# Weight sums of the blocks in more buffers, and the second mixture's words moved behind the second sum and the first gate

## The chip, the cores and the metric

One core of a Trainium2 chip runs the kernel. The metric is device time in microseconds (us) of one execution, the median of three. The engines named below are TensorE (PE, the matmuls; PEld are its weight loads), VectorE (DVE), ScalarE (ACT), GpSimd (POOL) and SyncE (SP), which here only issues DMAs.

## The reference

Attention in chunks of 64 feeds a gated layer (the first mixture, `_moe_ref`), and that feeds a second layer with a softmax and a norm (`_moe2_ref`).

```python
x = attention(q, k, v)                    # 4608 tokens x 512
h = x @ w_in                              # 512 x 2048
g = h * np.clip(h + 3.0, 0.0, 6.0) / 6.0
x = g @ w_out                             # 2048 x 512
h = x @ w_in2                             # 512 x 1024
solu = h * softmax(h)
y = (solu - mean) / sqrt(var + 1e-6) * g_ln @ w_out2
```

## The kernel before

Float32 products are made of three matmuls on split operands: each operand is a high part `hi` (a cast to fp32r) and a low part `lo` (the rest), and hi*hi, lo*hi and hi*lo are summed in PSUM. The 4608 tokens are nine blocks of 512.

The first three blocks run the first mixture directly. In the loop over `F` (two blocks of 16 hidden chunks each, from about 112 us to 308 us of the profile), `moe_h` makes a hidden chunk, `moe_gate_there` gates it on DVE, `moe_split` splits it (ACT casts `g_hi`, DVE subtracts `g_lo`), and `o_next` multiplies the chunk before by `wo`. Attention of later blocks runs in the same loop. Beside them the loop prepares weights for the later blocks, which use a seven-product (Strassen-like) form. `sums_of(kind, j)` adds the halves of two weight tiles on DVE (line 1075, into `w[0]` and `w[1]`) and forms four sums on POOL (lines 1080 to 1083). Two passes later, `split_sums(kind, j, i)` casts `w[i]` on ACT into a high part (line 1089), subtracts on POOL (line 1090), and `store_sums` writes both parts to memory. The table `UNITS` says in which pass a unit starts: input weights ("i", j) in passes 0, 2, ... 14, output weights ("o", j) in 1, 5, 7 and then in 16 to 24.

The last six blocks are three pairs. The third, `pair`, runs from 640 us to 760 us of the profile, in eight iterations of j. An iteration makes seven products `mul7` (A11, S2, S1, S3, A12, A22, S4) and, from j = 1, two `o_next`. Its sums are `u2` (line 1522, from S2), `u3` and `c22` (1532, 1534), `c21` (1552, from A22) and `c12` (1558, from S4); `gated` makes a rectified copy on ACT (line 1230) and multiplies on DVE (line 550). S3 adds to the bank that `u2` reads, so it waits for `u2`; A22 in the same way waits for `u3`; A11 of the next iteration takes the bank that `gated(a)` reads; S2 of the next iteration takes the bank that `c21` reads.

`fill` (class `Second`) prepares the weights of the second layer inside the pair, in windows. A window of words waits for a raw chunk from memory (`fetch`, into `xr0` and `xr1` in turn), scales it on ACT (line 155) and joins its words on DVE (lines 258, 261 and, for `w_out2`, 267). Its small steps are DVE subtractions: `lo` parts (line 295) and differences (302). `hi` casts on ACT into a free place (line 319). The places are few: `wi14`, `wi15`, `pbd`, and `s3` with `xo3`. `fill.store()` issues the stores of finished parts from ACT's own queue (line 326); a cast into a place waits until the stores of what it held have landed. All engines run their instructions in the order of the program, and a DMA that an engine issues stands in that order too.

Of the kernel before, what the change touches and what calls it, by code (L numbers as in the profile page):

```python
# [8 lines left out]
F32 = mybir.dt.float32  # L9
# [7 lines left out]
P = 128  # L17
# [4 lines left out]
def tile_kernel(  # L22
# [15 lines left out]
    NT, DM = out.shape  # L38
# [28 lines left out]
    xrp = ctx.enter_context(tc.tile_pool(name="xr", bufs=1))  # L67
    ap1 = ctx.enter_context(tc.tile_pool(name="ap1", bufs=1))
# [8 lines left out]
    def work_tile(tag, dtype=F32, shape=(P, DM), name=None):  # L77
        i = turns[tag] % width[tag]
        turns[tag] = i + 1
        return wcp.tile(list(shape), dtype, tag=f"{tag}{i}", name=name or tag)  # L80
# [263 lines left out]
    def load_2(n):  # L344

        o, j = LOADS[n]
        if o == "out":
            homes = ((ap2, "v"), (ap2, "v")), ((ap2, "p"), (ap2, "p")), ((ap1, "q"), (ap1, "tx0")), ((ap1, "tx1"), (ap1, "tx2"))
            t = out_w[j] = [narrow(*h) for h in homes[j]]
            for i in range(2):  # L350
                nc.sync.dma_start(out=t[i].bitcast(F32), in_=st2[OPERANDS.index((o, j))][:, i])
        else:
            t = wi_slot(2 * XQ.index(o) + j, F32R)
            w2[o, j] = pair_of(t)
            nc.sync.dma_start(out=t.bitcast(F32), in_=st2[OPERANDS.index((o, j))])
# [23 lines left out]
    def att_psum():  # L379
        return ps_att.tile([P, 2, DM], F32, tag="att", name="att")  # L380
# [4 lines left out]
    def h_psum():  # L385
        return ps_h.tile([P, DM], F32, tag="h", name="hp")
# [162 lines left out]
    def moe_gate(hp, t):  # L549
        nc.vector.scalar_tensor_tensor(  # L550
            out=t, in0=t, scalar=6.0, in1=hp, op0=ALU.min, op1=ALU.mult
        )

    def moe_split(t, eng, between=None):
        g_hi = gp.tile([P, BT], F32R, tag="g_hi", name="g_hi")
        g_lo = gp.tile([P, BT], F32R, tag="g_lo", name="g_lo")
        nc.scalar.copy(out=g_hi, in_=t)  # L557
        if between:
            between()
        eng.tensor_sub(out=g_lo, in0=t, in1=g_hi.bitcast(F32))  # L560
        return g_hi, g_lo
# [503 lines left out]

    def sums_of(kind, j):

        if kind == "o" and j < 3:
            t = xrp.tile([P, 2, DM], F32, tag="xr0", name="xr0")
            w = [t[:, i] for i in range(2)]  # L1070
        else:
            w = [ap1.tile([P, DM], F32, tag=f"tx{i}", name=f"tx{i}") for i in range(2)]
        for i in range(2):
            t = (wi if kind == "i" else wo)[2 * j + i].bitcast(F32)
            nc.vector.tensor_add(out=w[i], in0=t[:, 0], in1=t[:, 1])
        k = slice(0, 2 * P), slice(2 * P, DM)
        (a11, a12), (a21, a22) = ([t[:, c] for c in k] for t in w)
        if kind == "o":
            a12, a21 = a21, a12
        nc.gpsimd.tensor_add(out=a22, in0=a21, in1=a22)  # L1080
        nc.gpsimd.tensor_sub(out=a21, in0=a11, in1=a21)
        nc.gpsimd.tensor_sub(out=a11, in0=a22, in1=a11)
        nc.gpsimd.tensor_sub(out=a12, in0=a12, in1=a11)
        summed[kind, j] = w
# [74 lines left out]
    def mul7(ps, j, wn, xname, start, stop):  # L1159
        w, (hi, lo) = ring_take(wn, j), xq[xname]  # L1160
        n = 0
        for i, x in ((0, hi), (1, hi), (0, lo)):
            for kk in range(2):
                nc.tensor.matmul(  # L1164
                    ps, w[:, i, kk * P : (kk + 1) * P], x[:, kk],
                    start=(start and n == 0), stop=(stop and n == 5), skip_group_check=True,
                )
                n += 1
        ring_fetch()
# [54 lines left out]
    def o_next():  # L1224
        if pend:
            moe_o(*pend.pop(0))

    def gated(h):
        t = gp.tile([P, BT], F32, tag="t", name="t")
        nc.scalar.activation(out=t, in_=h, func=AF.Relu, bias=three[:])  # L1230
        moe_gate(h, t)
        return t

    def load_h(f):
        h_t2[f] = work_tile("s")
        nc.sync.dma_start(out=h_t2[f], in_=held[f])
# [253 lines left out]
    def load_o(f):  # L1490
        j, i = divmod(f, 2)
        wo[f] = wo_slot(f, F32R)
        for c in range(2):
            nc.sync.dma_start(
                out=halves_of(wo[f][:, c]), in_=sto[4 + 2 * i : 6 + 2 * i, j, :, c].rearrange("s p c -> p s c")
            )

    def pair(p, todo):
        b1, b2 = FIRST + 2 * p, FIRST + 2 * p + 1
        hang, fill = None, second[0]  # L1500
        for j in range(NJ):
            lastj = j == NJ - 1
            if j == 1:
                width.update({"s": 3, "xo": 3})
                fill.places.append(3)
            for f in range(2 * j + ND, 2 * j + ND + 2):
                if f < NF:
                    load_o(f)
            a = att_psum()[:, 0]
            mul7(a, j, "A11", "B11", True, False)  # L1510
            s1 = work_tile("s")
            nc.scalar.copy(out=s1, in_=a)
            if hang:
                t, f = hang
                g = moe_split(t, nc.gpsimd)
                pend.append((b1, f, g))
            if j:
                fill.window(1, 0)
            b = h_psum()
            mul7(b, j, "S2", "T2", True, False)  # L1520
            u2 = work_tile("s")
            nc.vector.tensor_add(out=u2, in0=s1, in1=b)  # L1522
            while todo:
                todo.pop(0)()
            if j:
                fill.window(1, 2)
            c = h_psum()
            mul7(c, j, "S1", "T1", True, False)
            o_next()
            mul7(b, j, "S3", "T3", False, False)  # L1530
            u3 = ap1.tile([P, DM], F32, tag="tx2", name="tx2")
            nc.vector.tensor_add(out=u3, in0=s1, in1=b)
            c22 = work_tile("xo")
            nc.vector.tensor_add(out=c22, in0=u3, in1=c)
            if not lastj:
                nc.sync.dma_start(out=held[2 * j + 1], in_=c22)
            if not j:
                fill.window(1, 0)
            mul7(a, j, "A12", "B21", False, True)
            if lastj:  # L1540
                for n in range(4):
                    load_2(n)
                fetch_x2(0)
            fill.store()
            t = gated(a)
            g = moe_split(t, nc.gpsimd)
            o_next()
            pend.append((b1, 2 * j, g))
            fill.window(0, 2 * (j > 0), False)
            mul7(b, j, "A22", "T4", False, True)  # L1550
            c21 = ap1.tile([P, DM], F32, tag=f"tx{j % 2}", name=f"tx{j % 2}")
            nc.vector.tensor_add(out=c21, in0=s1, in1=b)
            mul7(c, j, "S4", "B22", False, True)
            if lastj:
                for n in range(4, 8):
                    load_2(n)
            c12 = work_tile("xo")
            nc.vector.tensor_add(out=c12, in0=u2, in1=c)
            if lastj:
                h_t2[2 * j], h_t2[2 * j + 1] = c12, c22  # L1560
                for f in range(2):
                    load_h(f)
            else:
                nc.sync.dma_start(out=held[2 * j], in_=c12)
            fill.store()
            hang = gated(c21), 2 * j + 1
            if not j:
                fill.window(1, 2)
        g = moe_split(hang[0], nc.vector)
        pend.append((b1, hang[1], g))  # L1570

        es_r.close()
        xp[0] = ctx.enter_context(tc.tile_pool(name="xp", bufs=2, reuse_waits="tile"))
        width.update({"s": 4, "xo": 4})
        order = [NF - 1, NF - 2] + list(range(NF - 2))
        nxt = gated(h_t2.pop(order[0]))
        for i, f in enumerate(order):
            t = nxt
            if i == 1:
                o_next()  # L1580
            if i + 1 < NF:
                nxt = gated(h_t2.pop(order[i + 1]))
            if i != 1:
                o_next()
            g = moe_split(t, nc.vector)
            pend.append((b2, f, g, i))
            if i + 4 < NF:
                load_h(order[i + 4])
            end_work(i)
        flush()  # L1590
# [31 lines left out]
    for f in range(NF):  # L1622
# [4 lines left out]
        hp, t = moe_h(f, *xn[0])  # L1627
# [49 lines left out]
    for F in range(2 * NF):  # L1677
        b, f = 1 + F // NF, F % NF
        if F == 0:
            xn[2] = new_x()  # L1680
        hp, t = moe_h(f, *xn[b])
# [170 lines left out]
```

## Time and profile before

| | us |
|---|---|
| median of three runs (lowest, highest) | 1187.03 (1186.27, 1187.85) |
| the profiled execution's own time | 1183.92 |
| its span, first to last instruction | 1181.8 |
| PE busy in the span | 1167.3 |
| DVE, ACT, POOL busy | 886.8, 726.5, 490.9 |

The span is 2.1 us shorter than the profiled execution's time, and that time is 3.1 us below the median of the runs. Busy PE is 99% of the span, at a granted clock of 1.000 of full speed throughout.

### The profile page before, as it was taken

The page shows a single profiled execution, that of the slowest core. Times are in us where ns is not written, and L with a number is a line of the kernel's source. Part 1 is how long each engine was busy: PE and PEld are TensorE (multiplying, and loading weights), DVE is VectorE, ACT ScalarE, POOL GpSimd, SP SyncE. Part 2 cuts the span into 40 slices and gives each one's busy share as a digit, 9 for nine tenths or more (in the row PEclk, how much of TensorE's full clock was granted, in tenths as well). Part 3 has the DMA queues.
Part 4 walks back from the last instruction along what each step waited for, and adds up shares of the span by engine and source line. Part 5 has one row for each costly group of instructions (what it writes and reads, how often), then busy time and mean ns, then how long its engine had stood idle before and what let it go on. Part 6 is the DMA issues. An engine that isn't in the chain of part 4 may idle for free.

```text
span 1181.8 us, 21412 instructions
## 1 busy us (share of the span) xinstructions
PE 1167.3 (99%) x7199; PEld 949.8 (80%) x7199; DVE 886.8 (75%) x1415; ACT 726.5 (61%) x1669; POOL 490.9 (42%) x565
## 2 busy tenths in 40 slices
PE   8999999999999999999999999999999999999998
PEld 6888777788878888888887778888888888888887
DVE  7987767677577987577867757768887878787774
ACT  7775445555465773466644333447887868677775
POOL 1000565443066710276400112101677666766764
PEclk9999999999999999999999999999999999999999
DMA  9901768687689998899999999871323232222321
GB/s 358 399 28 55 241 213 270 231 279 248 230 289 304 320 372 284 256 310 300 328 314 359 382 391 379 315 235 56 126 77 97 74 92 79 86 85 73 98 63 57
DMA packets 172253, 258.60 MB, mean 219 GB/s; under 512 B 19056, under 2 KB 86896, under 8 KB 172144
## 3 DMA queue, kind: packets, MB, share of 16 engines
q1 hardware_dynamic: 159760, 234.69, 57.8%
q10 hardware_dynamic: 12384, 22.55, 5.4%
q8 instruction: 57, 0.93, 0.3%
q14 instruction: 52, 0.43, 0.1%
HBM read 170.40 MB, written 76.02 MB: 209 GB/s over the span
## 4 chain that ended last, share of the span: by engine, by line
PE 86%; DMA 5%; DVE 4%; POOL 1%; ACT 1%; issue 1%; SPq 0%; ACTq 0%; POOLq 0%; DVEq 0%
PE po L949 17%; PE acc L574 14%; PE acc L1302 9%; PE hp L535 9%; PE acc L1164 8%; PE hp L1164 6%; PE b L751 6%; PE hp L1302 4%; PE c L751 4%; PE a L751 4%; PE att L398 3%; DMA xr<-in_moe_w_out 2%; PE att L751 1%; PE att L1164 1%; DMA wo<-sto 1%
## 5 line engine op out<-in xcount | busy, mean ns | idle before, releaser
L574 PE MATMUL acc<-g_hi,wo 128*128 128x512 f32 x640 | 163.1, 394 | 0.4 <-ACT g_hi L557 0.4
L574 PEld LDWEIGHTS acc<-g_hi,wo 128*128 128x128 f32 x640 | 118.8, 188 | 27.1 <-ACT g_hi L557 0.8
L1164 PE MATMUL hp<-wi,w 128*128 128x512 f32 x468 | 117.2, 393 | 3.2 <-DVE s L1522 2.9
L1164 PEld LDWEIGHTS hp<-wi,w 128*128 128x128 f32 x468 | 87.3, 188 | 24.9 <-DVE s L1522 4.4
L1164 PE MATMUL acc<-wi,w 128*128 128x512 f32 x420 | 104.4, 395 | 0.0
L864 ACT COPY wo<-wo 32x256 f32<-32x256 f32 x228 | 92.1, 404 | 18.1 <-DVE wo L846 10.2
L535 PE MATMUL hp<-x_hi,wi 128*128 128x512 f32 x384 | 97.9, 396 | 0.1
L1302 PE MATMUL acc<-wi,w 128*128 128x512 f32 x408 | 95.3, 392 | 0.0
L732 POOL TENSOR_TENSOR x_lo<-xr,x_hi 128x768 fp32r<-128x768 f32 (+1 forms) x30 | 63.8, 2149 | 75.5 <-ACT x_hi L725 72.6
L1164 PEld LDWEIGHTS acc<-wi,w 128*128 128x128 f32 x420 | 78.0, 188 | 17.2
L1302 PEld LDWEIGHTS acc<-wi,w 128*128 128x128 f32 x408 | 76.5, 188 | 16.8
L448 ACT ACTIVATE p<-att,mx 128x64 f32<-128x64 f32 x256 | 76.5, 321 | 20.4 <-DVE mx L431 17.6
L574 PE MATMUL acc<-g_lo,wo 128*128 128x512 f32 x320 | 87.6, 389 | 0.0
L535 PEld LDWEIGHTS hp<-x_hi,wi 128*128 128x128 f32 x384 | 71.5, 187 | 17.3 <-ACT x_hi L512 0.3
L1286 DVE TENSOR_TENSOR wi<-wo,wi 128x1024 fp32r<-128x1024 f32 x50 | 66.2, 1343 | 22.3 <-ACT wi L1285 21.8
L1285 ACT CAST wi<-wo 128x1024 fp32r<-128x1024 f32 x50 | 51.4, 1064 | 33.4 <-PE hp L1302 16.6
L836 DVE SCALAR_TENSOR_TENSOR wo<-wo,r,wo 128x1024 f32<-128x1024 f32 x36 | 69.4, 1929 | 1.3
L574 PEld LDWEIGHTS acc<-g_lo,wo 128*128 128x128 f32 x320 | 60.1, 188 | 12.8
L933 POOL TENSOR_TENSOR wo<-wo,wo 128x1024 fp32r<-128x1024 f32 x25 | 63.9, 2555 | 6.6 <-ACT wo L929 5.1
L560 POOL TENSOR_TENSOR g_lo<-t,g_hi 128x512 fp32r<-128x512 f32 x15 | 21.4, 1427 | 102.9 <-ACT g_hi L557 75.6
L541 ACT ACTIVATE t<-hp,three 128x512 f32<-128x512 f32 x48 | 33.2, 692 | 40.7 <-PE hp L535 38.3
L828 ACT ACTIVATE wo<-wo,nmx 128x1024 f32<-128x1024 f32 x36 | 41.5, 1152 | 24.1 <-DVE nmx L825 24.0
(319 smaller groups left out, 2847.1 us busy)
## 6 DMA issues: line engine op xcount, KB each, us to landing
w<-sti SPq DMA_DIRECT2D x168, 256.0 KB, 5.0
w<-sto SPq DMA_DIRECT2D x112, 256.0 KB, 4.8
later_t<-xo SPq DMA_DIRECT2D x48, 256.0 KB, 4.7
wo<-later_t SPq DMA_DIRECT2D x24, 512.0 KB, 5.7
wo<-wo SPq DMA_DIRECT2D x328, 32.0 KB, 1.8
x2d<-xo SPq DMA_DIRECT2D x36, 256.0 KB, 4.1
xr<-x2d SPq DMA_DIRECT2D x36, 256.0 KB, 3.4
out<-ob SPq DMA_DIRECT2D x36, 256.0 KB, 2.2
```

Of the source, the lines that this page charges most:

```text
L448: nc.scalar.activation(out=p_t[u][:, h], in_=sc[:, c, a], func=AF.Exp, scale=0.125, bias=mx[:, m : m + 1], accum_out=sums[u][:, h : h + 1],)
L535: nc.tensor.matmul(hp, wi[f][:, a, kk * P : (kk + 1) * P], b[:, kk], start=(n == 0), stop=(n == 3 * KD - 1),)
L574: nc.tensor.matmul(acc[dc], wo[f][:, w, dc * P : (dc + 1) * P], g[i], start=(at == 0 and n == 0), stop=(at == NF - 1 and n == 2),)
L732: eng.tensor_sub(out=lo[:, f], in0=r, in1=hi[:, f].bitcast(F32))
L751: nc.tensor.matmul(ps, x[:, AT[a], j], w2[w, j][i], start=(start and n == 0), stop=(stop and n == 5), skip_group_check=True,)
L836: nc.vector.scalar_tensor_tensor(out=h, in0=e, scalar=r, in1=h, op0=ALU.mult, op1=ALU.mult, accum_out=mu)
L864: move(out=m[b * 32 : b * 32 + 32, a], in_=tr[a * 32 : a * 32 + 32, b])
L933: eng.tensor_sub(out=lo, in0=m, in1=hi.bitcast(F32))
L949: nc.tensor.matmul(po, a[f], out_w[f][w], start=(n == 0), stop=(n == 3 * NF2 - 1),)
L1164: nc.tensor.matmul(ps, w[:, i, kk * P : (kk + 1) * P], x[:, kk], start=(start and n == 0), stop=(stop and n == 5), skip_group_check=True,)
L1286: nc.vector.tensor_sub(out=e[1], in0=src, in1=e[0].bitcast(F32))
L1302: nc.tensor.matmul(ps[s], w[:, k, s * P : (s + 1) * P], x[l], start=(start and j == 0 and n == 0), stop=(stop and j == NJ - 1 and n == 2), ...
```

## The change

Two parts. In the blocks, `sums_of` takes other buffers: an input unit with odd j takes `xr1` (one tile of two halves), one with even j takes `tx2` and `tx1`, and output units from j = 3 take `tx0`, `tx1` or `tx2`, `tx1` in turn; before, all of these took `tx0` and `tx1`. In the last pair, the windows and the stores change places: from j = 1 the first window of words comes behind `u2` instead of ahead of the product S2, the second comes behind `gated(a)`, the second `o_next` and the first `fill.store()` instead of behind `u2`, and the window of two small steps without words moves to the end of the iteration. At the end, the gate of c21 comes ahead of the second `fill.store()`.

```diff
     def sums_of(kind, j):
 
-        if kind == "o" and j < 3:
-            t = xrp.tile([P, 2, DM], F32, tag="xr0", name="xr0")
+        tag = "xr0" if kind == "o" and j < 3 else "xr1" if kind == "i" and j % 2 else None
+        if tag:
+            t = xrp.tile([P, 2, DM], F32, tag=tag, name=tag)
             w = [t[:, i] for i in range(2)]
         else:
-            w = [ap1.tile([P, DM], F32, tag=f"tx{i}", name=f"tx{i}") for i in range(2)]
+            tags = ("tx0", "tx1") if j % 2 else ("tx2", "tx1")
+            w = [ap1.tile([P, DM], F32, tag=t, name=t) for t in tags]
...
-            if j:
-                fill.window(1, 0)
             b = h_psum()
             mul7(b, j, "S2", "T2", True, False)
...
             if j:
-                fill.window(1, 2)
+                fill.window(1, 0)
             c = h_psum()
             mul7(c, j, "S1", "T1", True, False)
...
-            if not j:
-                fill.window(1, 0)
             mul7(a, j, "A12", "B21", False, True)
...
-            fill.store()
             t = gated(a)
             g = moe_split(t, nc.gpsimd)
             o_next()
             pend.append((b1, 2 * j, g))
-            fill.window(0, 2 * (j > 0), False)
+            fill.store()
+            fill.window(1, 2)
             mul7(b, j, "A22", "T4", False, True)
...
+            hang = gated(c21), 2 * j + 1
             fill.store()
-            hang = gated(c21), 2 * j + 1
-            if not j:
-                fill.window(1, 2)
+            fill.window(not j, 2, False)
```

The number of instructions on PE, DVE and ACT stays the same. The first place is DVE in the blocks, where the sums of passes 4 to 8 stand (other rows lie between these). The number behind a tag is a buffer's own; a wait on Pool is one for POOL's last reading of a buffer. Before:

```order
L1075 TENSOR_TENSOR tx0_1810<-wi4_570 128x512 [waits Pool_49]
L1075 TENSOR_TENSOR tx1_1811<-wi5_620 128x512
L1075 TENSOR_TENSOR xr0_1907<-wo2_569 128x512
L1075 TENSOR_TENSOR tx0_1965<-wi6_669 128x512 [waits Pool_49]
L1075 TENSOR_TENSOR tx1_1966<-wi7_728 128x512
L1075 TENSOR_TENSOR xr0_2072<-wo4_668 128x512 [waits Pool_49]
L1075 TENSOR_TENSOR tx0_2132<-wi8_780 128x512 [waits Pool_49]
```

And of the change:

```order
L1077 TENSOR_TENSOR tx2_1809<-wi4_570 128x512 [waits Pool_49]
L1077 TENSOR_TENSOR tx1_1810<-wi5_620 128x512
L1077 TENSOR_TENSOR xr0_1906<-wo2_569 128x512 [waits Pool_49]
L1077 TENSOR_TENSOR xr1_1964<-wi6_669 128x512 [waits Pool_49]
L1077 TENSOR_TENSOR xr0_2070<-wo4_668 128x512 [waits Pool_49]
L1077 TENSOR_TENSOR tx2_2130<-wi8_780 128x512
```

Each input unit now writes a buffer that the input unit before it does not hold, so that the reading it waits for is that of an older unit; the three output units of passes 1, 5 and 7 still share `xr0`.

The second place is ACT in iteration j = 2 of the last pair, from the copy of `s1` to the rectified copy of c21 and the next copy of `s1`. Waits on DMAHW are waits for a DMA to land. Before:

```order
L319 CAST pbd_7860<-kbd_7456 128x512 [waits DMAHW5_49,DMAHW3_49]
L155 ACTIVATE xr0_7724<-xr0_7724 128x512 [waits DMAHW1_49]
L319 CAST wi15_7880<-v_7458 128x512
L319 CAST wi14_7882<-p_7460 128x512 [waits DMAHW2_49,DMAHW0_49,DVE_49]
L326 DMA st2<-s_7857 128x512 [waits DMAHW3_49,Activation_49]
L1230 ACTIVATE t_7930<-att_7836,three_59 128x512 [waits PE_49,Pool_49]
L557 CAST g_hi_7933<-t_7930 128x512 [waits DVE_49]
L326 DMA st2<-wi15_7880 128x512 [waits DMAHW4_49,Activation_49]
L326 DMA st2<-wi14_7882 128x512 [waits DMAHW0_49,Activation_49]
L1230 ACTIVATE t_7976<-tx0_7959,three_59 128x512 [waits DVE_49,Pool_49]
L1512 COPY s_7994<-att_7985 128x512 [waits PE_49]
```

And of the change (here as above, only the first of the stores of one part is shown, but for `pbd`):

```order
L319 CAST s_7860<-v_7455 128x512 [waits DMAHW5_49]
L1232 ACTIVATE t_7907<-att_7828,three_59 128x512 [waits PE_49,Pool_49]
L557 CAST g_hi_7910<-t_7907 128x512 [waits DVE_49]
L326 DMA st2<-pbd_7792 128x512 [waits DMAHW1_49,Activation_49]
L326 DMA st2<-pbd_7792 128x512 [waits DMAHW3_49]
L155 ACTIVATE xr0_7788<-xr0_7788 128x512 [waits DMAHW2_49]
L319 CAST pbd_7937<-v_7454 128x512 [waits DMAHW3_49,DMAHW1_49]
L319 CAST wi15_7939<-kbd_7452 128x512 [waits DMAHW7_49,DMAHW5_49,DVE_49]
L1232 ACTIVATE t_7962<-tx0_7949,three_59 128x512 [waits DVE_49,Pool_49]
L326 DMA st2<-s_7860 128x512 [waits Activation_49]
L326 DMA st2<-wi14_7863 128x512 [waits DMAHW0_49,Activation_49]
L1514 COPY s_7986<-att_7977 128x512 [waits PE_49]
```

One scale of words (line 155) has moved behind the gate and behind four stores, and the cast into `pbd` now stands directly behind the stores of what `pbd` held.

The third place is DVE in the same iteration. Before:

```order
L258 TENSOR_SCALAR q_7457<-xr1_7680 128x512
L261 SCALAR_TENSOR_TENSOR q_7457<-xr1_7680,q_7457 128x512
L267 TENSOR_SCALAR q_7457<-q_7457,g_sb_60 128x512
L1522 TENSOR_TENSOR s_7871<-s_7845,hp_7862 128x512
L258 TENSOR_SCALAR p_7460<-xr0_7724 128x512
```

And of the change, from the same sum `u2` to `c21`:

```order
L1522 TENSOR_TENSOR s_7852<-s_7837,hp_7843 128x512
L258 TENSOR_SCALAR p_7456<-xr1_7676 128x512
L1534 TENSOR_TENSOR xo_7896<-tx2_7894,hp_7865 128x512
L550 SCALAR_TENSOR_TENSOR t_7907<-t_7907,att_7828 128x512
L258 TENSOR_SCALAR kbd_7452<-xr0_7788 128x512
L261 SCALAR_TENSOR_TENSOR kbd_7452<-xr0_7788,kbd_7452 128x512
L295 TENSOR_TENSOR xo_7861<-v_7455,s_7860 128x512
L295 TENSOR_TENSOR wi14_7863<-kbd_7452,wi14_7863 128x512
L1550 TENSOR_TENSOR tx0_7949<-s_7837,hp_7843 128x512
```

No words stand ahead of `u2` any more, and the second chunk's words and two low parts stand between the first gate (line 550) and `c21` (line 1550).

## Rows read from the trace of the kernel before

**Rows 1.** The page: busy time, share of the span, instructions.

```profile
PE 1167.3 (99%) x7199; PEld 949.8 (80%) x7199; DVE 886.8 (75%) x1415; ACT 726.5 (61%) x1669; POOL 490.9 (42%) x565
```

**Rows 2.** Windows: stretch, length, busy of each engine, granted clock, DMA share, GB/s.

```profile
118.00:310.00 192.00, 189.89 (x1549) 152.00 (x1548) 138.31 (x243) 99.50 (x341) 88.72 (x96) 1.00 0.69 233
...
641.00:700.00 59.00, 55.52 (x238) 44.05 (x238) 37.76 (x59) 22.48 (x37) 9.52 (x7) 1.00 1.05 385
700.00:765.00 65.00, 64.80 (x284) 53.06 (x283) 43.64 (x69) 26.92 (x45) 11.88 (x9) 1.00 0.97 358
```

**Rows 3.** What PE waited for, 118 to 310 us: total, times, longest.

```profile
PE att L398 <- DVE pbd L494: 1.7, 2, 1.2
PE acc L574 <- ACT g_hi L557: 0.4, 1, 0.4
```

**Rows 4.** Timeline of PE in the blocks: start, length, operation.

```profile
154.14 2.03 PE L535 MATMUL hp<-x_hi,wi 128*128 128x512 f32 x8
...
166.54 2.03 PE L535 MATMUL hp<-x_hi,wi 128*128 128x512 f32 x8
...
181.11 2.03 PE L535 MATMUL hp<-x_hi,wi 128*128 128x512 f32 x8
...
194.33 2.03 PE L535 MATMUL hp<-x_hi,wi 128*128 128x512 f32 x8
```

**Rows 5.** What DVE waited for, 112 to 310 us.

```profile
DVE tx L1075 <- POOL xo L1090: 25.2, 12, 3.6
```

**Rows 6.** Timeline of DVE in the blocks; in brackets, idle time before and its releaser.

```profile
160.41 1.29 DVE L1075 TENSOR_TENSOR tx<-wi 128x512 f32<-128x512 f32 x2 [3.53 <-POOL xo L1090]
...
175.67 1.29 DVE L1075 TENSOR_TENSOR tx<-wi 128x512 f32<-128x512 f32 x2 [3.57 <-POOL xo L1090]
```

**Rows 7.** What PE waited for, 641 to 765 us.

```profile
PE hp L1164 <- DVE s L1522: 2.9, 3, 1.8
```

**Rows 8.** Timeline of PE in the last pair: starts of A11 (att), the last products, the tail.

```profile
639.68 1.54 PE L1164 MATMUL att<-wi,w 128*128 128x512 f32 x6
...
649.94 1.66 PE L1164 MATMUL att<-wi,w 128*128 128x512 f32 x6 [0.47 <-DVE t L550]
...
682.07 1.54 PE L1164 MATMUL att<-wi,w 128*128 128x512 f32 x6
...
699.33 1.54 PE L1164 MATMUL att<-wi,w 128*128 128x512 f32 x6
...
744.99 1.54 PE L1164 MATMUL att<-wi,w 128*128 128x512 f32 x6
...
757.29 2.91 PE L1164 MATMUL hp<-wi,w 128*128 128x512 f32 x12
760.04 1.98 PE L574 MATMUL acc<-g_hi,wo 128*128 128x512 f32 x8
```

**Rows 9.** Timeline of DVE in the last pair.

```profile
689.03 1.30 DVE L261 SCALAR_TENSOR_TENSOR v<-xr,v 128x512 int32<-128x512 int32 x1 [0.86 <-ACT xr L155]
690.25 0.68 DVE L1522 TENSOR_TENSOR s<-s,hp 128x512 f32<-128x512 f32 x1
```

**Rows 10.** Timeline of ACT in the last pair; ACTq rows are DMAs that it issues.

```profile
667.57 0.83 ACTq L326 DMA_DIRECT2D st<-wi  x2
...
675.45 0.62 ACT L319 CAST wi<-p 128x512 fp32r<-128x512 f32 x1 [0.61 <-DMA st<-wi]
...
682.46 3.76 ACTq L326 DMA_DIRECT2D st<-wi  x4
686.32 0.72 ACT L1230 ACTIVATE t<-tx,three 128x512 f32<-128x512 f32 x1 [4.12 <-issue]
```

**Rows 11.** The stores of line 326, 641 to 765 us: from issue to landing.

```profile
DMA to landing us min/median/max: 2.2/5.3/7.4
```

**Rows 12.** The same, of the one store issued at 741.8 us.

```profile
DMA to landing us min/median/max: 3.0/3.0/3.0
```

**Rows 13.** What SP's queue waited for, 641 to 765 us.

```profile
SPq L1494 <- DMA w<-sti: 9.4, 12, 2.1
```

## Prediction

> **What bounds the kernel now.** I read the page's busy line first: PE is busy for 1167.3 of the span, 99% [rows 1]. So only PE's idle time can be won, and where PE is idle is the first question. The windows by stage answer it: in the blocks 192.00 us hold 189.89 of busy PE, so 2.1 are idle; in the first 59.00 of the last pair 55.52 are busy, so 3.5 are idle, and in the rest of the pair 0.2 [rows 2]. The granted clock is 1.00 in all three. By the busy line alone no more than about 5.8 us could be won in the two places that the diff touches.
>
> Then I read what PE waits for. In the blocks the waits that are named add to 2.1 [rows 3], in the pair one line stands out, S2 (hp, line 1164) waiting for the sum `u2` of line 1522 [rows 7]. The waits of the other engines tell why: DVE waits 25.2 us in twelve pieces for POOL to finish reading a sum [rows 5], and ACT and DVE each wait for words and stores of the second mixture [rows 9, 10]. Because modelled ends of matmuls hide short waits, I cost the waits from starts of equal groups on PE's timeline [rows 4, 8]. They come to somewhat more than the windows show.
>
> All is reckoned against the profiled execution of 1183.92 us; the median, 1187.03, is 3.1 above it, and I carry the difference to the median. 0.2% of it, 2.4 us, is about what a measurement of this kernel can tell from no change.
>
> **Blocks, what is removed: -3.0.** Two passes of the loop take 166.54 - 154.14 = 12.40 where nothing is late. The next two take 181.11 - 166.54 = 14.57, the two after that 194.33 - 181.11 = 13.22 [rows 4]: 2.17 and 0.82 more, 2.99 together. In just these stretches DVE stands 3.53 and 3.57 us ahead of its line 1075 for POOL's subtraction of line 1090 [rows 6], and the gates, transposes and split parts behind it on DVE come late to PE. The reason is the buffer: `tx0` is written again while POOL still reads the unit before. After the change each input unit writes a buffer that the unit before it does not hold, so POOL's reading there has two passes more, some 12 us, against a stall of 3.6. The output units of passes 1, 5 and 7 still share `xr0` and still wait for POOL; those waits are earlier in POOL's order than the ones removed, and `xr1` is read last in pass 16, so nobody new is late. The bounds are -3.0 and nothing (if the waits only move); I take -3.0, since the rows tie the loss to this one releaser.
>
> **Pair, the old waits: -5.4.** The last two products, six matmuls each, take 760.04 - 757.29 = 2.75, so seven take 9.62. The last iteration takes 760.04 - 744.99 = 15.05 from its A11 to the tail [rows 8], and is my base; it leaves (15.05 - 9.62) / 2 = 2.71 for an `o_next`. From A11 to A11 the others take: j = 0, which has no `o_next`, 10.26, that is 0.65 over 9.62, with 0.47 of it shown as a wait for the gate; j = 1 and 2 together 32.13, 2.03 over twice 15.05; j = 3 17.26, 2.21 over; j = 4 to 6 45.66, 0.51 over [rows 8]. The sum is 5.4. What is late is told by DVE and ACT: line 261 waits 0.86 for ACT's scale and then takes 1.30, and `u2` starts right behind it, at 690.25, while S3 needs the bank that `u2` reads [rows 9]. The words no longer stand ahead of `u2`, and in j = 0 the first gate no longer stands behind casts, so I take all of it; the bounds are -5.4 and, by the busy PE of the windows, -3.7 [rows 2].
>
> **Pair, the new waits: +5.5 (0.8 to 10).** Now four or two stores, a scale, the words' line and two low parts stand between the first gate and `c21`. Let E be the end of A12. The bank of `c21` is wanted by the next S2 at E + 6.85 (`o_next` 2.71, A22 and S4 2.75, A11 half of that, 1.37). On ACT and DVE: relu 0.72 and a cast 0.62 [rows 10] and the gate 0.7, near the sum of 0.68 on DVE [rows 9]: E + 2.0; issues at 0.42 each [rows 10], with four stores to E + 3.7; then the scale, line 261, two low parts and `c21`, five of about that same length, 3.4: E + 7.1, or 0.6 more where POOL slows line 261 to its 1.30 [rows 9]. So with four stores (j = 2, 3, 6) PE waits at least 0.25 to 0.9 each: that is the lower bound, 0.8 as a round sum of the three at the low end.
>
> The larger part is a round trip. The cast into a place stands directly behind the stores of what it held, and waits until they have landed. It happens twice per iteration, and between the trips stand relu and gate. A trip is the fourth issue 1.3 later, the landing, 5.3 at the median [rows 11], and a cast of 0.6: 7.2. Two trips and relu of c21 0.7, relu of a 0.7, gate 0.7 and `g_hi` 0.6 make 17.1 us for ACT, against 15.05 for PE: +2.1 in each of j = 2 and 3, where both trips have four stores; the trip of j = 1 makes the next `u2` about 1.0 late, that of j = 6 0.3: 5.5. For it speaks that before, with relu, the gate and other stores between a store and the cast into its place, a cast still waited 0.61, and that four issues took 3.76 and held a relu for 4.12 [rows 10]. With a landing of 3.0, as a store takes in the calm stretch at 741.8 [rows 12], the loop is 12.5, no bound, and the floors alone stay. With 6.35, halfway from the median to the longest of 7.4, the loop is 19.3: 4.3 twice and 1.4 make 10. I take the median, as the DMA share of this stretch is 1.05 [rows 2].
>
> The Trainium skill ("DMA: Bandwidth & Descriptors", section "Anatomy of one DMA — SWDGE (gpsimd) path") has a price for a landing: on GpSimd's path it fits a DMA as 2.0 us and its bytes over 436 GB/s, which makes an estimate of 2.6 us for a store of 256 KB, and by it the round trips would cost only the floors. The trace's median of 5.3 [rows 11] does not agree, the lone store of 3.0 [rows 12] nearly does.
>
> **Pair, the tail: +2.0 (1.3 to 3.0).** In j = 7 the last cast into `wi15` stands on ACT between the stores of `wi15` and the relu of c21. With a landing of 3.0 the cast ends at E + 6.6, relu 7.3, gate 8.0, two low parts 9.3, `g_lo` 10.0; with 5.3 `g_lo` ends at 11.7. PE wants it in the third matmul of its last `o_next`, at about E + 8.7. Late by 1.3 or 3.0; 2.0 is between; the store nearest in time is the one of [rows 12]. Nothing of before stands at this place [rows 8].
>
> **At no cost.** The tags add no instruction. The fetch of the second chunk (about 1 MB) is issued later, behind A12; its reader has moved as far, some 7 us, which covers it. It passes the weight loads in SP's queue, where twelve waits of 2.1 at most stand already [rows 13]; the ring of tiles loaded ahead covers those. If that cover is gone, a load's wait is PE's.
>
> **Sum.** -3.0 - 5.4 + 5.5 + 2.0 = -0.9: 1183.0 for the execution profiled, a median of 1186.1.
>
> **Rivals.**
> (1) Faster: the stores land fast. Fewer transfers lie on each other since the stores are spread, and rows at either end exist [rows 11, 12]. -3.0 - 5.4 + 0.8 + 1.3 = -6.3: 1180.7. With a landing of 4.5 about -3.6, 1183.4. Chance 0.34 for all of this side.
> (2) Slower: late stores hold SP too. DMAs of both queues take turns on a few semaphores (the DMAHW numbers in the listing of the change), so that a DMA can only be issued when the one before it on its semaphore has landed; SP's rows show such waits, 9.4 us in twelve [rows 13]. A store that waits in ACT's order would hold SP's loads, which hold ACT's next store. Then the new waits come to their upper bound 10 and the tail to 3.0: -8.4 + 13.0 = +4.6, 1191.6. It decides from where both new terms together exceed 8.4 + 2.4 = 10.8. Against it: no such SP wait was longer than 2.1. Chance 0.20.
> (3) The blocks' part does not do what it says: DVE waits for POOL at `xr0` instead, as the output units keep one buffer. The -3.0 goes: +2.1, 1189.1. Rows 6 show waits at input units alone, so 0.06.
>
> **The numbers.** The forecast itself has 0.40, and about 3 us to each side; of it 0.12 end faster by over 0.2%, 0.24 within, 0.04 slower. Rival 1 is faster but for 0.02, rival 2 slower but for 0.02, rival 3 within but for 0.01. That makes 0.44, 0.33 and 0.23. The range leaves out a tenth at either end: the lowest of rival 1 and the upper half of rival 2, so 1181.0 to 1190.5.
>
> **What the profile would show.** Blocks: pairs of passes of 12.40 throughout, no wait of PE for `pbd` or `g_hi`, DVE's waits for POOL at line 1077 well under 25.2. Pair: no wait of PE for `u2` behind words; new waits of S2 for `c21` (line 1550), of ACT's casts (line 319) for stores, two an iteration and several us long in j = 2 and 3; iterations of 17 in these two and near 15.05 in others; in the tail a wait of line 574 for the last gate. The prediction is wrong if ACT's casts wait little (then rival 1), if SP's waits grow to several us each (rival 2), or if the pairs of passes keep their 14.57 (rival 3).

## The result, and the profile after

| | before | changed |
|---|---|---|
| median of five runs, us (lowest, highest) | 1186.27 (1184.91, 1187.85) | 1197.03 (1196.29, 1198.89) |
| the profiled execution's own time, us | 1183.92 | 1196.29 |
| its span, us | 1181.8 | 1194.5 |

The changed kernel is slower: the ratio is 1.0093, 95% interval 1.0078 to 1.0108, about 11 us. The forecast was 1186.1, and its range ended at 1190.5.

The page's busy line answers to [rows 1], and the windows (stretch, length, busy of each engine, granted clock, DMA share, GB/s) to [rows 2]; the last window is new.

```profile
PE 1172.9 (98%) x7199; PEld 953.9 (80%) x7199; DVE 898.6 (75%) x1415; ACT 727.0 (61%) x1669; POOL 494.6 (41%) x565
```

```profile
118.00:310.00 192.00, 191.83 (x1560) 154.12 (x1560) 150.03 (x247) 102.40 (x344) 93.65 (x96) 1.00 0.71 239
641.00:700.00 59.00, 54.83 (x230) 43.49 (x228) 36.99 (x56) 20.38 (x34) 9.66 (x7) 0.97 1.01 368
700.00:765.00 65.00, 62.03 (x263) 50.11 (x263) 39.44 (x60) 22.43 (x37) 11.17 (x8) 0.97 0.88 313
765.00:785.00 20.00, 13.81 (x52) 10.62 (x51) 14.04 (x25) 10.76 (x17) 0.00 (x0) 0.83 0.68 247
```

The blocks won: idle PE falls there from 2.1 us to 0.2. The pair and its tail lost in the other three windows, in idle time and in clock, which is below 1.00 in each of them. PE's starts on its timeline give the sum; they answer to [rows 8], where A11 of j = 0 began at 639.68.

```profile
636.95 1.54 PE L1166 MATMUL att<-wi,w 128*128 128x512 f32 x6
...
646.56 1.54 PE L1166 MATMUL att<-wi,w 128*128 128x512 f32 x6
...
678.65 1.54 PE L1166 MATMUL att<-wi,w 128*128 128x512 f32 x6
...
688.73 2.93 PE L1166 MATMUL hp<-wi,w 128*128 128x512 f32 x6 [2.18 <-DVE s L1522]
691.46 1.85 PE L1166 MATMUL att<-wi,w 128*128 128x512 f32 x6
...
698.61 1.54 PE L1166 MATMUL att<-wi,w 128*128 128x512 f32 x6
...
708.48 2.37 PE L1166 MATMUL hp<-wi,w 128*128 128x512 f32 x6 [2.17 <-DVE s L1522]
710.66 2.43 PE L1166 MATMUL att<-wi,w 128*128 128x512 f32 x6
...
718.41 1.54 PE L1166 MATMUL att<-wi,w 128*128 128x512 f32 x6
...
748.53 1.54 PE L1166 MATMUL att<-wi,w 128*128 128x512 f32 x6
...
764.27 1.98 PE L574 MATMUL acc<-g_hi,wo 128*128 128x512 f32 x8
...
773.34 1.22 PE L574 MATMUL acc<-g_hi,wo 128*128 128x512 f32 x2 [6.19 <-ACT g_hi L557]
...
777.53 0.62 PE L574 MATMUL acc<-g_hi,wo 128*128 128x512 f32 x2
...
783.67 1.08 PE L751 MATMUL att<-wi,x_hi 128*128 128x512 f32 x4
```

The last of these groups, the first of line 751, stood here before:

```profile
770.92 1.08 PE L751 MATMUL att<-wi,x_hi 128*128 128x512 f32 x4
```

Up to the pair the kernel gained 639.68 - 636.95 = 2.73. From there to the tail's first `o_next` it took 764.27 - 636.95 = 127.32 against 120.36 before: 6.96 lost. From there to line 751 it took 19.40 against 10.88: 8.52 lost. The sum, 12.75, is the whole difference of the spans, 12.7.

What PE and ACT waited for in the pair and its tail, 641 to 784 us (total, times, longest), shows who is late:

```profile
ACT pbd L319 <- DMA st<-pbd: 21.7, 5, 6.1
ACT wi L319 <- DMA st<-wi: 9.3, 5, 3.6
...
PE acc L574 <- ACT g_hi L557: 6.2, 1, 6.2
...
PE hp L1166 <- DVE s L1522: 4.4, 2, 2.2
...
ACT s L319 <- DMA st<-s: 3.7, 3, 2.2
PE hp L1166 <- DVE tx L1550: 2.8, 5, 0.8
```

Of PE's waits only the five for `c21` (line 1550, 2.8) are of the kind for which the sum had a lower bound. The larger ones are for `u2` and for the last gate. ACT waits 34.7 us at line 319 for stores to land, and once 5.1 at its copy of `s1` (line 1514). ACT's timeline at three places shows both:

```profile
684.91 0.62 ACT L319 CAST wi<-kbd 128x512 fp32r<-128x512 f32 x1 [2.45 <-DMA st<-wi]
...
702.21 0.33 ACTq L326 DMA_DIRECT2D st<-s  x1
703.36 0.33 ACTq L326 DMA_DIRECT2D st<-xo  x1
704.06 3.02 ACTq L326 DMA_DIRECT2D st<-wi  x2
707.12 0.58 ACT L1514 COPY s<-att 128x512 f32<-128x512 f32 x1 [5.14 <-DMA st<-s]
...
760.70 0.62 ACT L319 CAST pbd<-kbd 128x512 fp32r<-128x512 f32 x1 [6.06 <-DMA st<-pbd]
761.23 0.68 ACT L1232 ACTIVATE t<-att,three 128x512 f32<-128x512 f32 x1
...
762.67 0.83 ACTq L326 DMA_DIRECT2D st<-wi  x2
...
770.62 0.62 ACT L319 CAST wi<-p 128x512 fp32r<-128x512 f32 x1 [3.57 <-DMA st<-wi]
```

The cast at 684.91 has waited for the stores of its place; the rectified copy of `c21`, the gate and two low parts stand behind it and ahead of `u2`, which is late in j = 3. In j = 4 it is another wait. At 702.21 four stores are issued. They are spread over 4.9 us, and the copy of `s1` stands behind them, though A11 is long done; `u2` needs `s1`. No cast is in this row, so none waits for its place: the stores wait to be issued. The semaphores in the trace tell for what. The DMAs of both queues take eight semaphores in turn, and none of the 36 stores is issued before the DMA that had its semaphore last has landed. The last of the four, at 706.76, has that of a weight load that SP issued at 700.70 and that took 6.0 us to land. Of the 36 stores 24 come so behind a DMA of SP's and 12 behind one of ACT's own. In the tail a cast waits 6.06 for a landing, holds the gate of `a`, and a second cast waits for stores that are issued only after it; the last gate comes behind both.

### The profile page after: what moved, and what is told of

It is laid out like the page before. It is cut to its first block, busy times and chain, and to the rows that moved or that the text cites. A ratio compares the mean times of both kernels' runs of the same rounds, so it can differ in the third digit from the quotient of the medians.

```text
span 1194.5 us, 21394 instructions
## 1 busy us (share of the span) xinstructions
PE 1172.9 (98%) x7199; PEld 953.9 (80%) x7199; DVE 898.6 (75%) x1415; ACT 727.0 (61%) x1669; POOL 494.6 (41%) x565
## 4 chain that ended last, share of the span: by engine, by line
PE 86%; DMA 8%; ACT 2%; DVE 2%; issue 1%; POOL 1%; ACTq 0%; SPq 0%; POOLq 0%; DVEq 0%
PE po L949 16%; PE acc L574 15%; PE hp L535 10%; PE acc L1304 9%; PE acc L1166 8%; PE hp L1166 6%; PE b L751 6%; PE hp L1304 4%; PE c L751 4%; PE a L751 4%; PE att L398 3%; DMA st<-wi 2%; DMA st<-pbd 2%; DMA w<-sti 1%; PE att L751 1%; PE att L1166 1%
```

## The experiments

Two theories were set against each other and against a rival. **Trips**: a cast into a place waits until the stores of what it held have landed. **Turns**: a store waits to be issued until the DMA that had its semaphore before, the one eight DMAs earlier and mostly one of SP's, has landed; ACT stands meanwhile. **Order**, the rival: the words, low parts and issues themselves stand ahead of `c21` and the gates. All ratios are to the kernel before, run on the same chip; 0.1% is about 1.2 us.

| run | ratio | 95% interval |
|---|---|---|
| changed kernel | 1.0093 | 1.0078 to 1.0108 |
| e1_blocks | 0.9977 | 0.9965 to 0.9988 |
| e5_pair | 1.0134 | 1.0120 to 1.0148 |
| e2_const | 1.0042 | 1.0027 to 1.0056 |
| e7_sp | 1.0053 | 1.0040 to 1.0067 |
| e8_sp_const | 0.9967 | 0.9955 to 0.9979 |
| e3_tail | 1.0055 | 1.0040 to 1.0069 |
| e4_first | 0.9982 | 0.9969 to 0.9994 |
| e9_blocks_sp | 0.9987 | 0.9978 to 0.9996 |
| e10_first_sp | 0.9981 | 0.9971 to 0.9990 |
| e13_blocks_const | 0.9965 | 0.9952 to 0.9978 |
| e11_near | 1.0025 | 1.0014 to 1.0037 |
| e12_near_sp | 0.9951 | 0.9939 to 0.9963 |

**The two parts by themselves.** e1_blocks is the diff's first part (`sums_of`) alone, e5_pair all the rest alone.

> Kernel before with the blocks' part of the change alone (other buffers for the weight sums). If the two parts don't touch each other, the blocks begin the last pair 2.7 us earlier, as the changed kernel's trace shows (A11 of j = 0 at 636.95 against 639.68), and the whole is 2.7 us faster than before, ratio 0.998. If the earlier start is given back in the pair, where words and stores wait for transfers that did not become earlier, it is 0 to -1 us.

> Kernel before with the pair's part of the change alone. If the parts add, it is what the whole change lost plus what the blocks' part won: 10.8 + 2.7 = 13.5 us slower than before, ratio 1.0114. If the blocks' part makes the pair worse (its transfers then run 2.7 us earlier against the same stores), it is 10.8 slower or less.

The blocks' part wins 0.23%, 2.7 us, as its 2.73 in the trace. What DVE still waited for POOL there, 112 to 310 us of that run, answers to [rows 5]:

```profile
DVE xr L1077 <- POOL xo L1092: 1.4, 1, 1.4
```

The pair's part loses 1.34%; the sum of the parts would be 1.16% by the first two rows of the table. With the intervals of both rows taken in, the two are not clearly apart, so a small interaction stays open; that one part wins and the other loses does not.

**The landings taken away, the issues kept.** e2_const, on the changed kernel:

```diff
-                    nc.scalar.dma_start(out=st2[OPERANDS.index(name)][:, i], in_=t[i].bitcast(F32))
+                    nc.scalar.dma_start(out=st2[OPERANDS.index(name)][:, i], in_=xq["B22"][i][:, 0].bitcast(F32))
```

> Changed kernel in which every store of line 326 reads a high and low part that nobody writes in the pair, so that a cast into a place no longer waits for the stores of what the place held; number, size and order of the transfers stay. It leaves out the second layer's true weights. Theory trips (ACT stands at casts until stores have landed, and all behind it is late): the casts' waits of 34.7 us go, u2 is no longer late in j = 3 and 4, the tail's 6.2 us fall to about 1.3, no lower clock; only c21's five waits of 2.8 us stay: -2.7 - 5.4 + 3.4 + 1.3 = 3.4 us faster than before. Rival order (the words, the low parts and the issues ahead of c21 and of the gate make it late, whatever the landings): it stays within 2 us of the changed kernel, some 9 to 11 slower than before.

Neither theory has its number. Trips forecast 3 us faster, order 9 to 11 slower; it is 0.42% slower, some 5 us. The tail is as trips had it: of the wait of 6.2 for the last gate 0.4 is left, and 0.4 for its low part. In j = 3 and 4 PE has new waits, the longest of them these:

```profile
702.33 4.26 PE L1166 MATMUL hp<-wi,w 128*128 128x512 f32 x12 [2.61 <-DVE tx L1550]
...
712.07 1.66 PE L1166 MATMUL hp<-wi,w 128*128 128x512 f32 x6 [2.40 <-DVE s L1522]
```

ACT's timeline tells what for:

```profile
704.09 6.58 ACTq L326 DMA_DIRECT2D st<-wi  x4
710.71 0.59 ACT L1514 COPY s<-att 128x512 f32<-128x512 f32 x1 [7.61 <-DMA st<-wi]
```

Four issues take 6.58, and no cast waits for a landing any more. The scale ahead of `c21` stood 4.06 behind the issues of j = 3 in the same way (it starts at 699.09). That made the second theory, turns, and the next two runs test it.

**The issues taken off ACT; then both.** e7_sp, on the changed kernel, and e8_sp_const with the edit of e2_const as well:

```diff
-                    nc.scalar.dma_start(out=st2[OPERANDS.index(name)][:, i], in_=t[i].bitcast(F32))
+                    nc.sync.dma_start(out=st2[OPERANDS.index(name)][:, i], in_=t[i].bitcast(F32))
```

> Changed kernel with the stores of line 326 issued from SP's queue instead of ACT's; casts still wait for their landing. Theory turns (a store in ACT's order waits for the DMA eight before it, mostly a load of SP's, so ACT stands at the issue itself): ACT's waits at the issues go, and with them u2's lateness in j = 4 (2.2 us and its lower clock, 1.8): some 7 us slower than before. Theory trips (landings alone): as the changed kernel, 10 to 11 slower. Rival: the stores now hold SP's loads and PE waits for weights (ring or wo): more than 11 slower.

> As the run before, and the stores read parts that nobody writes in the pair (the second layer's true weights are left out), so ACT waits neither at the issues nor for landings. Theories trips and turns together: u2 is nowhere late, c21 by the 2.8 us of its five short waits, the tail by 0.7: about 3 us faster than before. Rival order (place of words and low parts on DVE): more than 5 us slower than before, as with the run that took away the landings alone.

With SP's queue alone 0.53% is lost, the 7 us that turns expected within its interval. With both away the kernel is 0.33% (3.9 us) faster than before, where some 3 us were expected. So each wait by itself holds ACT, and taking away one leaves most of the time to the other: against the changed kernel the landings away give 0.51%, the issues away 0.40%, both together 1.26%. PE's waits in the pair and tail of e8_sp_const, but for one of 0.3 at line 751:

```profile
PE hp L1166 <- DVE tx L1550: 1.0, 2, 0.6
PE acc L574 <- DVE g_lo L560: 0.4, 1, 0.4
PE acc L574 <- ACT g_hi L557: 0.4, 1, 0.4
```

The words and low parts stand on DVE just where the change put them, and `u2` is late nowhere. The rival order is out as the cause of the loss; it keeps the short waits for `c21`.

**The tail.** e3_tail, on the changed kernel: the second window of j = 7 makes no casts, and they come into the last loop; the stores behind the gate of c21 of j = 7 come behind that gate's split.

```diff
-            fill.window(1, 2)
+            fill.window(1, 2, not lastj)
...
+            if i == 3:
+                fill.hi()
+                fill.window(0, 2, False)
```

> Changed kernel, but the two casts that stand ahead of the last gate in j = 7, and their two low parts, come into the last stage's loop over i, behind i = 3. Theory trips: the last gate no longer waits for a landing; of the tail's 8.5 us (6.2 of wait, 2.2 of lower clock behind it) about 8 go, and it is some 2.7 us slower than before. The waits of j = 3 and 4 stay as they are. Rival: the last gate is late because its sum c21 stands behind words on DVE: then 4 us or more of wait stay at line 574 and it is 6 us or more slower than before.

Half a miss: 0.55% is lost where 2.7 us (0.23%) were forecast. The tail takes 777.09 - 762.10 = 14.99 in place of 19.40, so 4.4 go and not 8. The start of the tail, the wait that stays, and then its cause on ACT:

```profile
762.10 1.98 PE L574 MATMUL acc<-g_hi,wo 128*128 128x512 f32 x8
...
767.18 1.19 PE L574 MATMUL acc<-g_hi,wo 128*128 128x512 f32 x2 [2.20 <-ACT g_hi L557]
...
777.09 1.08 PE L751 MATMUL att<-wi,x_hi 128*128 128x512 f32 x4
```

```profile
758.66 0.62 ACT L319 CAST pbd<-kbd 128x512 fp32r<-128x512 f32 x1 [6.13 <-DMA st<-pbd]
```

The first trip of the iteration, behind `u2`, makes the gate of `a` late, and with it all that follows to the last gate. Both trips of j = 7 had their share in the tail.

**The order of before, with one thing changed each.** All have the blocks' part. e4_first moves the first window behind `u2`; e9_blocks_sp issues the stores from SP; e10_first_sp does both; e13_blocks_const stores parts that nobody writes.

> Blocks' part, and in the last pair of before one thing moved: the first window of words comes behind u2, just ahead of the second window; stores and the second window stay as before. Theory trips: the old waits of S3 for u2 (2.9 shown, 4 with their restarts) go and no cast comes nearer to the stores of its place, so 2.7 + 3 to 5 us faster than before. Rival order (more words in a row on DVE hold u3 and the gate): it gains no more than the blocks' 2.7.

> Blocks' part, the last pair in the order of before, stores of line 326 from SP's queue. Theory turns: of ACT's idle time ahead of the gates in the pair of before (four issues took 3.76 and held one 4.12) the issues' share goes, words come earlier, and of the pair's 5.4 us some 2 to 4 go: 5 to 7 us faster than before. If the pair's old waits are the words' own place on DVE, it gains the blocks' 2.7 only; if SP's loads are held, less.

> Blocks' part, the last pair in the order of before but the first window of words behind u2, and stores from SP's queue. Words no longer hold u2 (theory order) and issues no longer hold ACT (theory turns); landings still hold casts (the run with SP's queue and the order of before showed one of 6.9 us in j = 2). 3 to 5 us faster than before; if u3 and the gate take over u2's lateness, as with ACT's queue, only the blocks' 2.7.

> Blocks' part, the last pair in the order of before, stores from ACT of parts that nobody writes (the second layer's true weights are left out): what the landings cost in the old order. By theory trips the old order keeps casts some way behind the stores, so they cost little: the blocks' 2.7 and at most 1.5 more. If the old order's 5.4 us are landings too, 5 us or more faster than before.

None can be told from e1_blocks by its interval. So the first expectations of e4_first, e9_blocks_sp and e10_first_sp failed, and each came out as the other case named with it, the blocks' part alone. e13_blocks_const, 0.35% or some 4 us faster, is as trips had it: in the old order landings cost little. The waits move: in e4_first those for `u2` are gone, and instead PE waits for `u3` in j = 1 and for the gate in j = 4.

```profile
660.88 3.03 PE L1166 MATMUL hp<-wi,w 128*128 128x512 f32 x12 [1.71 <-DVE tx L1533]
...
695.87 1.66 PE L1166 MATMUL att<-wi,w 128*128 128x512 f32 x6 [1.83 <-DVE t L550]
```

In e9_blocks_sp, from j = 3 on, A11 follows A11 at 15.05 to 15.07, the base, but in j = 2 a cast waits 6.87 for a store that SP had issued at 669.45, with words and `u3` behind it.

```profile
674.59 0.62 ACT L319 CAST s<-kbd 128x512 fp32r<-128x512 f32 x1 [6.87 <-DMA st<-s]
```

**Both waits away with the true weights.** e11_near, on the changed kernel: low parts and stores come right behind their casts (the second group behind the gate of `c21`), and the place freed longest ago is taken first. e12_near_sp issues the stores from SP as well.

```diff
-            i = min(self.places) if kept else max(self.places)
-            if kept and i == 3:
+            i = next((n for n in self.places if not kept or n != 3), None)
+            if i is None:
...
             if j:
-                fill.window(1, 0)
+                fill.window(1, 0, False)
+                fill.hi()
+                fill.window(0, 2, False)
+                fill.store()
...
-            fill.store()
-            fill.window(1, 2)
+            fill.window(1, 0, False)
+            fill.hi()
...
             hang = gated(c21), 2 * j + 1
+            fill.window(not j, 2, False)
             fill.store()
-            fill.window(not j, 2, False)
```

> Changed kernel with the low parts and their store right behind the casts (first group behind u2, second behind the gate of c21), and a place freed longest ago taken first, so that a store has some 15 us to land before the next cast into its place. Stores from ACT's queue. Theory trips is met, theory turns not: casts wait no more, but the issues hold ACT as in the run with parts that nobody writes (3.7 to 6.6 us for four), so 0 to 6 us slower than before. If turns cost little once no landing is waited for, as fast as the next run.

> As the run before, stores from SP's queue: both waits of ACT are taken away, with the true weights stored. Theories trips and turns together: as fast as the run that had both away by leaving the weights out, 3 to 7 us faster than before. If SP's loads are held by the stores: PE waits for weights in the pair, and the gain is the blocks' 2.7 or less.

Both came out as expected: 0.25% slower with the stores on ACT, 0.49% faster (5.8 us) with them on SP, by its interval faster than every other kernel here that stores the true weights. In e11_near no cast waits for a landing any more, but ACT's copy of `s1` stands behind four issues, and the transfer that ends the wait is one of SP's weight loads:

```profile
670.07 2.92 ACTq L326 DMA_DIRECT2D st<-wi  x4
673.03 0.59 ACT L1514 COPY s<-att 128x512 f32<-128x512 f32 x1 [2.81 <-DMA w<-sti]
```

In e12_near_sp PE's waits in the pair and the casts' waits for landings come to this, and from j = 3 on every iteration takes 15.05 or 15.06:

```profile
PE hp L1166 <- DVE tx L1535: 1.7, 1, 1.7
ACT pbd L319 <- DMA st<-pbd: 1.2, 1, 1.2
PE hp L1166 <- DVE tx L1553: 0.6, 1, 0.6
```

## Why the prediction was wrong

**Blocks: right.** -3.0 forecast, -2.73 in the trace and 0.23% by itself in e1_blocks. The 2.73 is of one execution each: in the twelve profiles that have this part A11 of j = 0 begins at 636.28 to 638.83, in the two without it at 639.18 and 639.68. Rival 3 is out.

**Old waits of the pair: right for what it names.** In j = 0 seven products take 646.56 - 636.95 = 9.61, the 0.65 is gone; e8_sp_const, with nothing on ACT to wait for, has no wait for `u2` at all. But moving words out of `u2`'s way alone wins nothing that can be measured (e4_first): its pair has other waits instead.

**New waits of the pair: this step failed, by its size.** +5.5 with an upper bound of 10 was forecast. By A11's starts and the base of 15.05 it was 12.3: 4.91 in j = 3 (698.61 - 678.65), 4.75 in j = 4 (718.41 - 698.61), and 2.7 in the others. The mechanism named (casts behind the stores of their place, ACT as the loop that is too long) is there: PE's two waits for `u2` are 2.18 and 2.17, where 2.1 was forecast for each of the two iterations with four stores, and without the landings 0.51% comes back (e2_const). Three things were left out of the term.

The first is `c21`: its waits, 2.8 in five, stood beside the trips as a lower bound of 0.8 and were not added to them. The second is the issue: the loop was summed with 0.42 for each, though the row beside it had four in 3.76 [rows 10]. That row was cited in favour of the term and not put into it. Here four stores took 4.87 from 702.21, and the runs show that this costs PE time: 0.40% from the changed kernel to e7_sp, and 0.74% from e11_near to e12_near_sp, where hardly a cast waits for a landing.

The third is the clock, for which the sum had no term. PE's two waits of 2.2 were followed by products at half the clock: 2.93 + 1.85 and 2.37 + 2.43 for two groups that take 1.65 + 1.53 behind a wait in e3_tail, 3.2 us in all. Not all of that is lost, since PE then waits less for what comes next. e3_tail is the same program up to j = 7, and its clock does not fall in the pair. Its A11 of j = 0, and its S2 of j = 4:

```profile
637.07 1.53 PE L1166 MATMUL att<-wi,w 128*128 128x512 f32 x6
...
699.55 3.03 PE L1166 MATMUL hp<-wi,w 128*128 128x512 f32 x12 [2.12 <-DVE tx L1550]
```

S2 waits 2.12 for `c21` here and 0.40 in the changed kernel. From A11 of j = 0 to the tail e3_tail takes 762.10 - 637.07 = 125.03 in place of 127.32. So by these two executions the clock cost about 2.3, and some 10 of the 12.3 are waits, as much as the forecast's upper bound.

**Tail: failed by its size.** +2.0 (1.3 to 3.0) was forecast, 8.5 measured. The second store took about 7 us from 763.1 to the cast at 770.62, not 3.0 to 5.3; the first trip, which was counted for the pair alone, started this one 2.4 late (the rectified copy of `a` began at 761.23, A12 ended at 758.80), and in e3_tail, without the second trip, a wait of 2.20 stays; and 2.1 is the clock again (773.34 to 777.53 for three groups that took 0.68 each before).

**The rivals.** Rival 2 came nearest in sum (1191.6), and its rule, that a DMA is issued when the one before it on its semaphore has landed, is in the trace. But it had the loss on the wrong engine. SP did wait for a store's landing, once for 4.2, yet PE waited for no weight load; it was ACT that stood, mostly behind SP's loads, and with the stores on SP the kernel lost less, not more.

The Trainium skill ("DMA: Bandwidth & Descriptors", section "Anatomy of one DMA — SWDGE (gpsimd) path") says that a wait on a semaphore takes place on the issuing sequencer, ahead of the dispatch. The runs agree: ACT's copy waited 7.61 behind four issues in e2_const. The same page of the Trainium skill (section "Issuing engines are not separate DMA queues") has it that starting DMAs from several engines saves only the sequencer's time to start them, usually small beside the DMA itself. Here that time was not small: four issues took 2.92 (e11_near) to 6.58 (e2_const) of ACT's time, and ACT or SP as the issuer is the whole difference of e11_near and e12_near_sp, 1.0025 against 0.9951.

## What to carry to other kernels

A store has two prices on the engine that issues it: the wait until it may be issued, and the wait of the next writer of its source; read both from the engine's timeline (the span of the issues, and the cast's releaser) before other work is moved behind them, and sum them at what the rows show together, not each at its best. A wait that was found as a lower bound is added to a larger one at another place, not replaced by it. When one of two such waits in the same order is taken away, the other may take most of its place, so an experiment that removes one shows less than its share: remove both before an explanation is given up. And a stall of PE can cost more than its length, in the clock of what follows.

## What the runs showed that was not expected

The lower clock does not follow from the length of one wait alone. The windows of the changed kernel (stretch, length, busy PE, granted clock, DMA share, GB/s) have half the clock right behind the wait of 2.18 and behind the tail's 6.19:

```profile
690.00:692.00 2.00, 2.00 (x6) 0.50 1.05 399
...
773.00:775.00 2.00, 1.66 (x3) 0.50 0.01 2
```

In e3_tail a wait of 2.22 at the same product was followed by a group at the full clock's length, as was the wait of 2.40 in e2_const:

```profile
707.53 1.65 PE L1166 MATMUL hp<-wi,w 128*128 128x512 f32 x6 [2.22 <-DVE s L1522]
```

What else decides was not tried. Half is 1.2 GHz of 2.4. The spread of one kernel's executions goes with the clock too: of e4_first's twelve, the four at a mean granted clock of 1.000 took 1179.98 to 1181.50 us, the four at 0.998 or less 1183.50 to 1186.15. So one profile shows one case of what a program's waits cost. The other surprise is how wide landings of equal stores lie in one kernel: 2.0 to 8.6 us, median 5.3, in the changed one, against 2.2 to 7.4 before [rows 11].
